# Loads reordered on one queue and stores moved to another in an mLSTM cell followed by a gelu MLP

## The chip, the cores and the metric

The kernel runs on one core of a Trainium2 chip. A core has TensorE (PE in the profile, with its weight loads as PEld), VectorE (DVE), ScalarE (ACT), GpSimd (POOL) and SyncE (SP), which here does nothing but issue DMAs. Matmuls read SBUF and write PSUM; the other engines move and change what lies there. The metric is the time of one execution on the device in microseconds. Four executions of the kernel before took 489.47 to 491.64 us, with a median of 490.15 us.

## What is computed

The first half is an mLSTM cell over 4 batches, 8 heads and 768 time steps, with heads of 40 elements. The second half is a two-layer MLP on the joined heads (3072 tokens of 320), with a sigmoid form of gelu between the layers:

```python
for t in range(S):
    m_new = np.maximum(f_gate[:, :, t] + m, i_gate[:, :, t])
    f_stab, i_stab = np.exp(f_gate[:, :, t] + m - m_new), np.exp(i_gate[:, :, t] - m_new)
    C = f_stab * C + i_stab * outer(vt, kt)
    n = f_stab * n + i_stab * kt
    y[:, :, t] = sigmoid(o_gate[:, :, t]) * (C @ qt) / np.maximum(np.abs(n @ qt), 1.0)
h = x @ w_in                       # 320 -> 2048
out = (h * sigmoid(1.702 * h)) @ w_out   # 2048 -> 320
```

The indices that broadcast the gates are left out here. The two weights arrive as 64-bit floats, and the kernel builds 32-bit ones from their bits.

## The kernel before

**Chunks.** Time is cut into six chunks `w` of 128 steps; within a chunk the recurrence is written as attention: scores of queries against keys (`scores`, L348 on TensorE), a weight matrix `wt` of gate products (`weights`), their product on VectorE (L350), values and the carried state (`values`, L360 and L365), the normalised output `y` (L380 to L390), its transpose into `xT` (`seam`, L399 on TensorE and the copy L400 on ScalarE), and the state's update (`new_states` L425, `carry` L433 and L435). The MLP then runs on the chunk's 512 tokens. While the MLP of chunk `w` runs on TensorE, the attention steps of chunk `w + 1` are put between its blocks, by the lists `blocks` and `stops` at the end of the kernel.

**The order is written by hand.** Each engine runs its instructions in the order in which the program lists them, and one that waits holds all behind it on that engine. The same holds for the DMAs issued on SP. Which instruction waits for what is worked out from the tiles that it reads and writes; a tile of a pool with two buffers (`o_sb`, say) can be written a third time only when the first one has been read.

**Loads.** Chunk 0 loads keys and queries as they lie and transposes them on TensorE. Later chunks load them in blocks of 32 rows (`load_blocks`, L117): 16 DMAs for the keys into `k_bl` and 16 for the queries into `q_bl`, eight of 64 KB and eight of 16 KB each. VectorE transposes those blocks (`transposes`, L302). `spread` (L317) copies a row of gate maxima from DRAM to all partitions of the four `wt` tiles. `load` (L105) fetches the o gates, v and k of a chunk with one DMA of 640 KB each.

**The weights** come in 20 pieces (`fetch`, L166): pieces 0 to 9 are `w_in`, 10 to 19 `w_out`, each in one to three DMAs. `convert` turns a piece into 32-bit floats with two instructions on ScalarE (L228, L229) and four on VectorE (L232 to L237). The table `beside` says at which step of chunk 0's MLP a piece is converted (`weights_in`) and which are fetched there, since their raw bits reuse the room of pieces converted before.

**The MLP of chunk 0** is plain: `up` (L458, L464) and, for the first two blocks, `full_rows` (L714, L737); the gelus are L468 and L765; then 16 blocks `down` (L561), for `n` = 0 to 3 and four batches. At `n` = 3 a batch is finished: VectorE copies PSUM into `o_sb` (L565) and SP stores it (L566). Block 12 to 15 are those four. From chunk 1 on, `up_fast` (L513, L541, with VectorE's sums L501 to L504 and adds L521) and `down_fast` (L610, L615, stores L619) compute the products with fewer matmuls, from sums of weights (`first_sums` L489, `weight_sums` L580) made beside chunk 0's MLP.

**The places that the change touches** are the start of the schedule (before `gate_out`), the step `j == 0` of chunk 0, the loads at `j == 4`, the place of `transposes(1, b)` among the `down` blocks, and the store in `down`.

Of the kernel before, what the change touches and what calls it, by code (L numbers as in the profile page):

```python
# [22 lines left out]
L = 128  # L23
# [11 lines left out]
def kernel(  # L35
# [12 lines left out]
    nc = tc.nc  # L48
    B, H, S, D = q.shape
# [44 lines left out]
    def load_gates(w):  # L94
        for dst, src in ((f_sb, f_gate), (i_sb, i_gate)):
            dst[w] = ld.tile([BH, L], FP, tag="fi", bufs=4, name="fi")
            nc.sync.dma_start(out=dst[w], in_=src[:, :, w * L:(w + 1) * L].rearrange("b h s -> (b h) s"))
# [10 lines left out]
    def load_blocks(w, which=slice(0, 2)):  # L108
        both = (k_bl, k), (q_bl, q)
        for dst, src in both[which] if isinstance(which, slice) else both[which:which + 1]:  # L110
            for two in range(2):
                for d in range(0, D, 32):
                    n = min(32, D - d)
                    r = two * 64 + d
                    for g in range(L // 32):
                        t = w * L + g * 32
                        nc.sync.dma_start(  # L117
                            out=dst[r:r + 32, :, g, 0:n],
                            in_=src[:, two:H:2, t:t + 32, d:d + n].rearrange("b j s d -> s (b j) d"))
# [36 lines left out]
    def fetch(n):  # L156
        if 6 <= n < 10:
            bits[n] = gp.tile([128, 512, 2], U32, tag="g", name="bits")
        else:
            room = xs if n == 19 else big[:, n if n < 6 else (n - 10) % 6, :]  # L160
            bits[n] = room.bitcast(U32).rearrange("p (a two) -> p a two", two=2)
        for r, c, src in pieces[n][1]:
            dst = bits[n][r, c].rearrange("p a two -> p (a two)")
            if len(src.shape) == 3:
                dst = dst.rearrange("p (j m) -> p j m", j=src.shape[1])
            nc.sync.dma_start(out=dst, in_=src)  # L166
# [18 lines left out]
    def keep_busy(n, pool=ps_a, tag="a"):  # L185
        p_idle = pool.tile([128, W], FP, tag=tag, name="p_idle")
        for _ in range(n):
            T.matmul(p_idle, idle, idle.unsqueeze(1).to_broadcast([128, 4, 128]), start=True, stop=True)
# [34 lines left out]
    def convert(n, engines="AV"):  # L223

        lo, hi, dst = bits[n][:, :, 0], bits[n][:, :, 1], pieces[n][0]
        dst_u = dst.bitcast(U32)
        if "A" in engines:
            A.activation(out=dst, in_=hi.bitcast(FP), func=AF.Abs)  # L228
            A.activation(out=lo, in_=lo, func=AF.Copy, scale=2.0 ** -29)  # L229
        if "V" not in engines:  # L230
            return
        V.tensor_scalar(out=dst, in0=dst, scalar1=HI_MIN, scalar2=HI_MAX, op0=OP.max, op1=OP.min)  # L232
        V.tensor_scalar(out=dst_u, in0=dst_u, scalar1=3, scalar2=0x3FFFFFFF, op0=OP.logical_shift_left,
                        op1=OP.bitwise_and)
        V.scalar_tensor_tensor(out=dst_u, in0=hi, scalar=0xC0000000, in1=dst_u, op0=OP.bitwise_and,
                               op1=OP.bitwise_or)
        V.tensor_tensor(out=dst_u, in0=dst_u, in1=lo, op=OP.add)  # L237
# [60 lines left out]
    def transposes(w, b):  # L298
        for bl, st, dst, name in ((k_bl, k_st, kT, "kT"), (q_bl, q_st, qT, "qT")):
            dst[w, b] = work.tile([128, NP, L], FP, tag=name, bufs=4, name=name)  # L300
            if w:
                V.transpose(out=dst[w, b].rearrange("p j t -> p (j t)"),  # L302
                            in_=bl[:, b * NP:(b + 1) * NP].rearrange("p j g c -> p (j g c)"))
                continue
            pt = ps_a.tile([128, NP, L], FP, tag="a", name="p_t")
            for p in range(NP):
                h = b * H + 2 * p
                T.transpose(pt[:, p, :], st[:, h:h + 2, :].rearrange("p a b -> p (a b)"), ident)
            if b == 0:
                keep_busy(1)  # L310
            A.copy(out=dst[w, b], in_=pt)
# [244 lines left out]
    def down(w, b, n):  # L556
        if n == 0:
            o_ps[w, b] = (ps_m if b < 2 else ps_x).tile([128, DM], FP, tag="mx"[b // 2], name="p_out")
        po = o_ps[w, b]
        for f in range(n * 4, n * 4 + 4):  # L560
            T.matmul(po, gs[w, f // 2][:, f % 2, b * L:(b + 1) * L], w_out_sb[:, f, :], start=(f == 0),  # L561
                     stop=(f == NF - 1))
        if n == NF // 4 - 1:
            o = op.tile([128, DM], FP, tag="o", name="o_sb")
            V.tensor_copy(out=o, in_=po)  # L565
            nc.sync.dma_start(out=out[b * S + w * L:b * S + (w + 1) * L, :], in_=o)  # L566

# [87 lines left out]
    def run(calls):  # L657
        for f, *args in calls:
            f(*args)


    def gate_out(b):
# [81 lines left out]
    def weights_in(n):  # L744
        done, ahead = beside.get(n, ((), ()))
        for p in done:
            convert(p)
        for p in ahead:
            fetch(p)
# [8 lines left out]
    for w in range(NW):  # L758
        more = w + 1 < NW
        for j in range(NF // 2):  # L760
            if w == 0 and j == 0:
                weights_in(0)
                for pair_ in range(2):
                    for i, g in enumerate(hidden_of(0, pair_)):
                        A.activation(out=g, in_=first[pair_][i], func=AF.Gelu_apprx_sigmoid)  # L765
            elif w == 0 and j % 2 == 0:
                weights_in(j // 2)
                up(j, j == 2)
            elif w and j % 4 == 0:
                up_fast(w, j, next_keys if more and j == 0 else None)  # L770
            if j == 0 and more:
                load(w + 1, "o")
            if w == 0 and j == 0:
                load_blocks(1, 0)
                spread(1)
            if w == 1 and j == 3:
                weight_sums(3)
            if more:
                if j == 4:
                    if w == 0:  # L780
                        load_blocks(1, 1)
                    load(w + 1, "v")
                    if w:
                        spread(w + 1)
                if j == (4 if w else 6):
                    load(w + 1, "k")
                if w and j == 3:
                    for b in range(2, 4):
                        transposes(w + 1, b)
            if w and j in (3, 7):  # L790
                hidden_sums(w, 0, (j // 4 * 2, j // 4 * 2 + 1), 1, 2)
                if j == 3:
                    hidden_sums(w, 0, (0, 1), 3, 4)
        side = attention(w + 1) if more else []
        if w == 0:

            blocks = [(lambda b=b, n=n: down(w, b, n)) for ns in ((0, 1), (2,), (3,)) for b in range(B) for n in ns]
            stops = (0, 1, 5, 7, 9, 11, 13, 15)
        else:
            blocks = down_fast(w, 0) + down_fast(w, 1)  # L800
            stops = (0, 1, 2, 4, 8, 10, 11, 12)
        for i, block in enumerate(blocks):
            if w == 0:
                weights_in(4 + i)
                if i == 0:
                    load_gates(2)
                if i == 2:
                    first_sums((0, 1))
                if i == 10:
                    load_blocks(2)  # L810
                for b in {2: (0, 1), 7: (2,), 9: (3,)}.get(i, ()):
                    transposes(1, b)
            elif w + 2 < NW and i == 0:
                load_gates(w + 2)
                load_blocks(w + 2)
            block()
            if i in stops and side:
                run(side.pop(0))
            if w == 1 and i == 1:
                weight_sums(2)  # L820
            if w:
                for at, c, *what in ((0, 0, (2, 3), 3), (1, 0, (2, 3), 4), (1, 1, range(4), 1),
                                     (5, 1, range(2), 2), (6, 1, range(2, 4), 2), (7, 1, range(4), 4)):
                    if i == at:
                        hidden_sums(w, c, *what)
                if i == 2 and not more:
                    hidden_sums(w, 1, range(4), 3)
            elif i in (12, 14):
                weight_sums(i // 2 - 6)
# [30 lines left out]
```

## Time and profile before

| | |
|---|---|
| median of 4 executions | 490.15 us (489.47 to 491.64) |
| profiled execution, its own time | 490.16 us |
| its span in the profile | 488.5 us |
| TensorE clock granted | 1.00 throughout |
| DMA over the span | 44.87 MB, 92 GB/s on average |
| DMA share, 0 to 40 us / 40 to 80 / 80 to 120 | 0.99 / 0.87 / 0.69 |

In the lines of the profile, a time is in microseconds from the start of the span, L-numbers are lines of the kernel, and `out<-in` are the names of the tiles. In a timeline the columns are start, length, engine, line, operation, tiles and count; a bracket at the end holds the idle time before the instruction and what ended it. In a table of waits each line is the engine, its tile and line, what it waited for, and then the total in microseconds, how often, and the longest. A wait for several things is put down to the one that came last by the profile; where the one named had long been done, it was another, often a DMA. SP's lines (SPq) are DMA issues: the length is that of the issue and not of the transfer.

### The profile page before, as it was taken

What the parts mean: (1) busy time and instruction counts of PE and PEld (TensorE: products, weight loads), DVE (VectorE), ACT (ScalarE), POOL (GpSimd) and SP (SyncE); (2) the same over time, 40 slices, a digit from 0 to 9 for tenths busy, and PEclk for the clock granted to TensorE, in tenths of its full rate; (3) what the DMA queues carried; (4) which work ended last, traced back from release to release, by engine and by line L of the source; (5) the groups of instructions that cost most, each with busy time, mean ns of one, the idle gap of its engine ahead of it and who ended that gap; (6) DMA issues with size and microseconds to landing.
All of it is one profiled execution on the core that took longest, in us unless ns stands there. A gap on an engine that the chain in (4) does not pass through costs nothing. (4 is left out here: it accounts for less than half of the span.)

```text
span 488.5 us, 10441 instructions
## 1 busy us (share of the span) xinstructions
PE 480.7 (98%) x4076; PEld 396.1 (81%) x4076; DVE 343.3 (70%) x855; ACT 221.2 (45%) x575; POOL 61.0 (12%) x103
## 2 busy tenths in 40 slices
PE   8999999999999999999999999999999999999997
PEld 4874456877688999787999877999977999977897
DVE  8789768887978965677776586686576786254831
ACT  6766766402458500476800474900364930255300
POOL 4030002231000340000322000232000120000000
PEclk9999999999999999999999999999999999999999
DMA  9999799663896200996100696300393000000000
GB/s 134 179 271 329 109 283 151 88 73 82 125 233 65 29 28 15 150 223 78 12 29 1 111 256 77 33 28 3 67 260 36 1 2 29 28 2 0 1 27 28
DMA packets 175953, 44.87 MB, mean 92 GB/s; under 512 B 164352, under 2 KB 169504, under 8 KB 175904
## 3 DMA queue, kind: packets, MB, share of 16 engines
q1 hardware_dynamic: 175904, 44.21, 48.5%
q8 instruction: 32, 0.52, 0.4%
q14 instruction: 17, 0.14, 0.1%
HBM read 40.17 MB, written 4.01 MB: 90 GB/s over the span
## 5 line engine op out<-in xcount | busy, mean ns | idle before, releaser
L610 PE MATMUL p_out<-w_out_sb,g 128*128 128x160 f32 x480 | 69.8, 301 | 0.0
L400 ACT COPY xT<-p_x 128x384 f32<-128x384 f32 x24 | 11.0, 480 | 127.3 <-PE p_x L399 127.3
L610 PEld LDWEIGHTS p_out<-w_out_sb,g 128*128 128x128 f32 x480 | 66.3, 190 | 0.9
L521 DVE TENSOR_TENSOR g<-p_u,g 128x256 f32<-128x256 f32 x80 | 33.7, 425 | 44.6 <-PE p_u L513 35.1
L518 ACT COPY g<-p_u 128x256 f32<-128x256 f32 x120 | 43.0, 377 | 43.7 <-PE p_u L513 39.5
L525 ACT ACTIVATE g<-g 128x256 f32<-128x256 f32 x120 | 42.3, 423 | 40.2 <-DVE g L521 40.2
L337 POOL TENSOR_SCALAR_AFFINE_SELECT wt<-wt 128x1024 f32<-128x1024 f32 x20 | 22.7, 1134 | 233.5 <-ACT wt L335 231.1
L615 DVE TENSOR_TENSOR o_sb<-o_sb,p_out 128x160 f32<-128x160 f32 x70 | 21.4, 318 | 42.2 <-PE p_out L610 41.8
L335 ACT ACTIVATE wt<-wt,cols 128x128 f32<-128x128 f32 x160 | 48.0, 391 | 0.0
L513 PE MATMUL p_u<-xT,w_in_sb 128*128 128x256 f32 x160 | 39.2, 383 | 0.3 <-DVE o_sb L565 0.3
L513 PE MATMUL p_u<-xs,big 128*128 128x256 f32 x160 | 37.9, 380 | 0.2 <-issue 0.2
L541 PE MATMUL p_v<-xT,w_in_x 64*128 64x512 f32 x80 | 37.2, 603 | 0.0
L541 PE MATMUL p_u<-xT,w_in_x 64*128 64x512 f32 x80 | 37.0, 602 | 0.0
L561 PE MATMUL p_out<-w_out_sb,g 128*128 128x320 f32 x128 | 36.2, 437 | 0.0
L350 DVE TENSOR_TENSOR wt<-p_s,wt 128x512 f32<-128x512 f32 x48 | 30.5, 684 | 7.5 <-POOL wt L337 5.5
L610 PE MATMUL p_out<-t,big 128*128 128x160 f32 x240 | 35.5, 301 | 0.0
L513 PEld LDWEIGHTS p_u<-xT,w_in_sb 128*128 128x128 f32 x160 | 29.6, 190 | 6.1 <-DVE o_sb L615 1.5
L513 PEld LDWEIGHTS p_u<-xs,big 128*128 128x128 f32 x160 | 29.9, 190 | 5.1 <-issue 0.6
L610 PEld LDWEIGHTS p_out<-t,big 128*128 128x128 f32 x240 | 33.3, 190 | 0.2
L561 PEld LDWEIGHTS p_out<-w_out_sb,g 128*128 128x128 f32 x128 | 23.8, 190 | 10.1 <-issue 0.5
L521 DVE TENSOR_TENSOR g<-p_v,g 128x256 f32<-128x256 f32 x80 | 29.8, 414 | 0.0
L541 PEld LDWEIGHTS p_v<-xT,w_in_x 64*128 64x128 f32 x80 | 14.1, 186 | 16.0 <-issue 16.0
(168 smaller groups left out, 862.2 us busy)
## 6 DMA issues: line engine op xcount, KB each, us to landing
wt<-m_row SPq DMA_DIRECT2D x20, 512.0 KB, 6.8
out_dram<-o_sb SPq DMA_DIRECT2D x24, 160.0 KB, 1.8
eo<-in_o_gate_dram SPq DMA_DIRECT2D x5, 640.0 KB, 5.5
v_st<-in_v_dram SPq DMA_DIRECT2D x5, 640.0 KB, 8.8
k_st<-in_k_dram SPq DMA_DIRECT2D x5, 640.0 KB, 11.8
big<-in_moe_w_in_dram SPq DMA_DIRECT2D x5, 512.0 KB, 7.0
k_bl<-in_k_dram SPq DMA_DIRECT2D x40, 64.0 KB, 2.7
q_bl<-in_q_dram SPq DMA_DIRECT2D x40, 64.0 KB, 2.7
```

The source lines that it names most:

```text
L335: A.activation(out=x[:, h, :], in_=x[:, h, :], func=AF.Exp, scale=-1.0, bias=cols[w][:, b * H + h:b * H + h + 1])
L337: G.affine_select(out=x, in_=x, compare_op=OP.is_ge, fill=0.0, base=0, pattern=[[0, H], [1, L]], channel_multiplier=-1)
L350: V.tensor_tensor(out=wt[w, b][:, :, i, :], in0=pw[i], in1=wt[w, b][:, :, i, :], op=OP.mult)
L400: A.copy(out=xT[w][:, :, b, :], in_=px)
L513: T.matmul(p[k][:, ts[t]], a[:, k // 2, k % 2 * 128:(k % 2 + 1) * 128], b, start=first, stop=True, skip_group_check=True)
L518: A.copy(out=g[k][i][:, ts[t]], in_=chain[k][:, ts[0]])
L521: V.tensor_tensor(out=g[k][i][:, ts[t]], in0=p[k][:, ts[pt]], in1=g[k][i][:, ts[t]], op=OP.add)
L525: A.activation(out=dst, in_=dst if src is None else src, func=AF.Gelu_apprx_sigmoid)
L541: T.matmul(p[k], w_in_x[r, k, :], x[r, 2, :], start=False, stop=True, skip_group_check=True)
L561: T.matmul(po, gs[w, f // 2][:, f % 2, b * L:(b + 1) * L], w_out_sb[:, f, :], start=(f == 0), stop=(f == NF - 1))
L610: T.matmul(po, a(f), b[:, f, :], start=(f == 0), stop=(f == NH - 1))
L615: V.tensor_tensor(out=dst, in0=x, in1=po, op=OP.add)
```

## The change

There are five edits. The keys of chunk 1 are loaded at the start, behind the first ten pieces of weights, instead of behind pieces 10 to 15. Its queries are loaded at step `j == 0`, before `spread(1)`, instead of at `j == 4`; the o gates of chunk 1 are loaded at `j == 4` instead of `j == 0`. The four stores of chunk 0 are issued by ScalarE and not by SP. Of the four first gelus, the two of the first block stand before the conversion of piece 5 (and the fetches of 10 to 15, which are on SP and not held by it), and the other two after it. Among the `down` blocks, the transposes of chunk 1 stand before `first_sums((0, 1))` and not after it, and at other blocks keep their place.

```diff
-            nc.sync.dma_start(out=out[b * S + w * L:b * S + (w + 1) * L, :], in_=o)
+            nc.scalar.dma_start(out=out[b * S + w * L:b * S + (w + 1) * L, :], in_=o)
...
     def run(calls):
         for f, *args in calls:
             f(*args)
+
+    load_blocks(1, 0)
...
             if w == 0 and j == 0:
-                weights_in(0)
                 for pair_ in range(2):
                     for i, g in enumerate(hidden_of(0, pair_)):
                         A.activation(out=g, in_=first[pair_][i], func=AF.Gelu_apprx_sigmoid)
+                    if pair_ == 0:
+                        weights_in(0)
...
-            if j == 0 and more:
+            if j == (0 if w else 4) and more:
                 load(w + 1, "o")
             if w == 0 and j == 0:
-                load_blocks(1, 0)
+                load_blocks(1, 1)
                 spread(1)
...
                 if j == 4:
-                    if w == 0:
-                        load_blocks(1, 1)
                     load(w + 1, "v")
...
                 if i == 0:
                     load_gates(2)
+                for b in {2: (0, 1), 7: (2,), 9: (3,)}.get(i, ()):
+                    transposes(1, b)
                 if i == 2:
                     first_sums((0, 1))
                 if i == 10:
                     load_blocks(2)
-                for b in {2: (0, 1), 7: (2,), 9: (3,)}.get(i, ()):
-                    transposes(1, b)
```

## The prediction

> **What bounds the kernel now.** I read the page first, then the waits by stretch, then the timelines of SP, VectorE and TensorE between 30 and 130 us.
>
> ```profile
> span 488.5 us, 10441 instructions
> ...
> PE 480.7 (98%) x4076; PEld 396.1 (81%) x4076; DVE 343.3 (70%) x855; ACT 221.2 (45%) x575; POOL 61.0 (12%) x103
> ...
> PE 14%; DVE 0%; issue 0%
> ```
>
> TensorE is busy for 98% of the span, and the chain that ended last is TensorE alone. What another engine saves is therefore worth only the TensorE time that it frees. Such time is found in two places. The waits of 60 to 90 us, and then those of 104 to 124 us, give them:
>
> ```profile
> DVE qT L302 <- DMA q_bl<-in_q_dram: 1.6, 1, 1.6
> ...
> PE p_s L348 <- DVE qT L302: 0.7, 1, 0.7
> ```
>
> ```profile
> DVE o_sb L565 <- PE p_c L425: 3.1, 1, 3.1
> ...
> PE p_u L513 <- DVE o_sb L565: 0.3, 1, 0.3
> ```
>
> The first: the second chunk's queries land late, their transpose waits, and the scores on TensorE wait 0.7 us. The second looks small, so I compare the same stage in two chunks on TensorE's timeline, from the first product of `up_fast` to the first of `down_fast`:
>
> ```profile
> 116.04 1.56 PE L513 MATMUL p_u<-xT,w_in_sb 128*128 128x256 f32 x6
> 117.95 0.70 PE L513 MATMUL p_u<-xT,w_in_sb 128*128 128x256 f32 x2 [0.35 <-DVE o_sb L565]
> ...
> 150.45 2.34 PE L610 MATMUL p_out<-w_out_sb,g 128*128 128x160 f32 x16
> ...
> 194.64 2.14 PE L513 MATMUL p_u<-xT,w_in_sb 128*128 128x256 f32 x8
> ...
> 226.74 2.34 PE L610 MATMUL p_out<-w_out_sb,g 128*128 128x160 f32 x16
> ```
>
> Chunk w=1 takes 150.45 - 116.04 = 34.41 us, chunk w=2 takes 226.74 - 194.64 = 32.10, and w=3 also 32.10 (270.92 to 303.02). So 2.31 us are lost in w=1, most of it inside matmuls that count as busy. VectorE's timeline says why, and SP's says what is behind it:
>
> ```profile
> 112.04 0.49 DVE L390 SCALAR_TENSOR_TENSOR y<-eo,den 128x320 f32<-128x320 f32 x1
> 115.60 0.49 DVE L565 COPY o_sb<-p_out 128x320 f32<-128x320 f32 x1 [3.07 <-PE p_c L425]
> ```
>
> ```profile
> 32.34 12.69 SPq L166 DMA_DIRECT2D big<-in_moe_w_out_dram  x14
> 45.18 0.38 SPq L105 DMA_DIRECT2D eo<-in_o_gate_dram  x1
> 45.60 14.56 SPq L117 DMA_DIRECT2D k_bl<-in_k_dram  x16
> 60.27 2.22 SPq L317 DMA_DIRECT2D wt<-m_row  x4
> 62.59 3.11 SPq L166 DMA_DIRECT2D big<-in_moe_w_out_dram  x5
> 66.79 10.77 SPq L117 DMA_DIRECT2D q_bl<-in_q_dram  x16
> ...
> 104.15 9.19 SPq L117 DMA_DIRECT2D q_bl<-in_q_dram  x16
> 113.44 4.82 SPq L566 DMA_DIRECT2D out_dram<-o_sb  x4
> ```
>
> The first output tile was copied at 106.07, but SP issues its store only at 113.44, behind the third chunk's query loads. It lands 2.1 us later, at 115.54. `o_sb` has two buffers, so the third copy (L565) starts at 115.60. The wait is put down to p_c, which the copy does not read; it is the store.
>
> **The stores.** Four DMA issues leave SP for ScalarE. An issue takes 0.33 to 0.43 us on SP; four on ScalarE are some 1.5 us, beside idle stretches of 6 to 7 us before its L400 copies. Each store now waits on ScalarE for its VectorE copy, and the copy of xT (L400) is queued behind it. The last store follows a VectorE copy that I put at 115 to 116; xT for that batch then comes at 115.9 to 117.3 instead of 115.27. Its first reader is VectorE's L501, behind `carry`, at 118, so this is covered; an xT after 118 would cost TensorE time one to one. No row shows what an issue costs on ScalarE; between nothing and 1 us, two to three times SP's, xT stays ahead of 118, and I take SP's 0.4.
> With stores issued at 108.5, the third copy could follow y at 112.5, and VectorE would reach L501 at 117.5 instead of 119.88. Its work then until the L521 adds (8.7 us) ends at 126.2, before TensorE wants them (126.4). All 2.31 us return: the upper end of the gain.
> One thing stands against it. SP never has more than eight transfers in flight: the piece issued at 32.34 left when the one eight before it (issued near 24.8, 7.3 us to landing) had landed, and those around it follow the same rule. If ScalarE's stores are counted in the same eight, the first must wait for the ninth query load of chunk 2, issued near 108.5 and 2.9 us to landing: 111.4. It lands at 113.5, VectorE is ahead by 115.6 - 113.5 = 2.1 us, and 2.0 us return. At worst the first store waits for the last query load (113.0 + 2.2 = 115.2) and lands at 117.3: a loss of about 1.8. I take -2.0.
> The Trainium skill (DMA: Bandwidth & Descriptors, "Issuing engines are not separate DMA queues") says that issuing from another engine saves only the sequencer's issue time, since all transfers share the same 16 DMA engines. By it the gain here is four issues of an SP that nobody waits for, 0, and the whole sum about -0.7. The row at 113.44 weighs more with me: what is saved is the place in line, 7 us.
>
> **The loads.** SP's order becomes: keys of chunk 1 (16), m_row, pieces 10 to 15 (14), queries (16), spread (4), pieces 16 and 17 (5), o gate, v, pieces 18 and 19, k. Bytes and count are the same; I work out landings.
> - Keys: the slots come free as the earlier pieces land, 31.0 to 41.3. The rest go at 0.53 to 0.57 us each (8.0 us for fifteen after 52.2; 9.15 for sixteen after 94.90): done near 46.5 to 47.
> - Pieces 10 to 15: 3.1 MB at the 380 GB/s of 64 to 70 us are 8 us, landings from 50.8 to 58. Piece 10's conversion on ScalarE moves from 49.60 to 50.8, piece 11's ends at 53.4, the gelu behind it (52.46) at 54.5. TensorE needs that PSUM at 56.8: nothing lost, 2.3 us of cover. Later conversions keep their times.
> - Queries: slots from 53.6, last issue near 63.4, landing 65.6 (79 before). Their transpose waits for no load.
> - Spread 63.5 instead of 60.27, so pieces 16 and 17 land 3.3 us later: piece 16 at 73.9 (70.6 before, where ScalarE waits 0.47). Its conversion stands on VectorE ahead of the transposes: 73.9 + 0.6 for the ScalarE half, + 2.4 for the VectorE half, + 1.3 for the first kT and qT gives 78.2. TensorE is ready at 79.16 and started at 79.86: **-0.7**. This needs piece 16 by 74.9.
> - The sums moved behind the transposes (L489, 1.22 + 1.99) end at 82.6. The score product on VectorE follows at 82.6 to 83.8 (81.13 to 82.33 before); TensorE wants it at 84.8. Covered by 1.0, else one to one. From there VectorE is full until 108 with about 0.6 to 2 us of slack against TensorE.
> - o gate and v, 160-byte packets, go at about 1000 per us (k: 4096 packets, 85.7 to 89.8): 8192 of them after piece 17 (its data end near 73.7) put v at 83.9 (83.8 before); needed at 84.8. Tanh waits for the o gate (79), and piece 17's conversion on ScalarE slips from 77.56 to 82.7, just in front of VectorE's need at 83.8.
> Piece 16 bounds it all. Earliest is 72, if no slot is ever late. Latest: pieces and queries take their whole old spells, 47 + 12.7 + 10.8 = 70.5, + 10.3 from spread to landing = 80.8. The low end is nearer, since the old spells hold waits for a backlog (6.6 us behind the o gate, 5.4 on earlier pieces) that is then not there.
>
> **Gelus before a conversion.** ScalarE's table load (1.28) starts at 33.9 instead of 35.39; the first gelus wait for TensorE (36.0), the conversion follows at 37.0. TensorE's start at 37.33 moves by at most 0.1; VectorE's conversion slips 0.6, covered by its wait of 0.59 at 49.16. I count -0.1 to +0.1, so 0.
>
> **Sum.** -2.0 - 0.7 = -2.7. The two overlap in part: the stores' time is set by SP's loads, not by TensorE, so with shared slots the 0.7 is given back at L521; with free ones both count (-3.0). I take -2.3. The profiled execution took 490.16 (span 488.5 and 1.7 around it), the median is 490.15: 490.15 - 2.3 = 487.85.
>
> **Rivals.**
> 1. *The stores gain nothing* (the pessimistic end above, or ScalarE held too long): then -0.7 at most, and a late v gives it back: 489.4 to 491. For it: the eight slots. Against: the store now has only loads before it that are issued by 109.
> 2. *Slower: piece 16 is late.* VectorE waits for it in front of the transposes, and the scores start 4.3 us after its landing. Past 75.6 each microsecond costs one; with the stores' 2.0 the balance is even at 77.6, and at 80.8 the sum is +3.2: 493.4. For it: eight slots filled with 32-row loads of 0.55 us each. Against: the same transfers in another order had all been issued by 83.9, so an order alone should move a piece by no more than what was put ahead of it.
> 3. *The order of loads is hidden entirely* (v or VectorE takes the 0.7 back) while the stores pay: -2.0, 488.15. This lies in the forecast's own range.
>
> **Numbers.** Forecast with rival 3: 0.58, from 486.9 (-3.2) to 488.6. Rival 1: 0.27. Rival 2: 0.15. A measurement here tells 0.3%, 1.47 us, from no change: faster below 488.68, slower above 491.62. So faster 0.58, same 0.27, slower 0.15. The range runs from 486.9 to 491.3; beyond lie most of rival 2 and a little below.
>
> **What would show it.** Right: stores issued by ScalarE between 108 and 112; the third L565 copy before 114; the w=1 stage near 32.1 to 32.5; no wait of L348 on qT; all after 150 shifted as a block. Wrong: ScalarE waiting on piece 16 past 75, TensorE waiting at L348 or L360 (v), a gelu waiting on pieces 10 or 11 near 53, or stores still issued after 113.

## The result and the profile after

The changed kernel takes 491.3 us (median of 46 executions, 488.07 to 494.83) against 490.26 us for the kernel before (70 executions, 489.05 to 496.38). The ratio is 1.0013, with a 95% interval of 0.9999 to 1.0027. The forecast was 487.85 us, a gain of 2.3. There was no gain. The profiled execution took 492.62 us, with a span of 490.9 and a mean granted clock of 0.996; the one before had 490.16, 488.5 and 1.000. In the experiments below, one execution of e1 (617.35 us) and one of e6 (551.26 us), at mean clocks of 0.754 and 0.852, are left out of every count and ratio.

The page of the changed kernel, span and busy times:

```profile
span 490.9 us, 10438 instructions
...
PE 481.5 (98%) x4076; PEld 398.0 (81%) x4076; DVE 342.7 (70%) x855; ACT 220.9 (45%) x575; POOL 61.7 (13%) x103
```

TensorE's waits between 50 and 124 us, its timeline at the places that the prediction named, and then two lines of the timeline before that the prediction does not show:

```profile
PE p_h L458 <- ACT g L468: 2.0, 1, 2.0
PE p_s L348 <- DVE qT L302: 1.3, 1, 1.3
```

```profile
58.96 5.40 PE L458 MATMUL p_h<-xT,w_in_sb 128*128 128x512 f32 x8 [1.96 <-ACT g L468]
...
69.75 2.32 PE L561 MATMUL p_out<-w_out_sb,g 128*128 128x320 f32 x8
...
84.50 1.16 PE L348 MATMUL p_s<-qT,kT 40*128 40x128 f32 x16 [1.34 <-DVE qT L302]
...
120.67 1.99 PE L513 MATMUL p_u<-xT,w_in_sb 128*128 128x256 f32 x8
...
152.90 2.34 PE L610 MATMUL p_out<-w_out_sb,g 128*128 128x160 f32 x16
```

```profile
65.74 2.32 PE L561 MATMUL p_out<-w_out_sb,g 128*128 128x320 f32 x8
...
79.86 1.16 PE L348 MATMUL p_s<-qT,kT 40*128 40x128 f32 x16 [0.70 <-DVE qT L302]
```

The first waits line is new, the second has nearly doubled (1.34 us against 0.70), and the wait of L513 for `o_sb` is gone. Read the starts against those before, in microseconds:

| place on TensorE | before | after | later by |
|---|---|---|---|
| first `down` block (L561) | 65.74 | 69.75 | 4.01 |
| first scores (L348) | 79.86 | 84.50 | 4.64 |
| first `up_fast` product of w=1 (L513) | 116.04 | 120.67 | 4.63 |
| first `down_fast` product of w=1 (L610) | 150.45 | 152.90 | 2.45 |
| end of the span | 488.5 | 490.9 | 2.4 |

So two things happened, of opposite sign. Up to the scores TensorE loses 4.6 us, and the w=1 stage gives back 2.18: it takes 152.90 - 120.67 = 32.23 us instead of 34.41. The difference of some 2.4 us stays to the end.

**The stores did what was forecast.** VectorE's and ScalarE's timelines, at the third output tile and at the stores:

```profile
116.67 0.49 DVE L390 SCALAR_TENSOR_TENSOR y<-eo,den 128x320 f32<-128x320 f32 x1
117.08 0.48 DVE L565 COPY o_sb<-p_out 128x320 f32<-128x320 f32 x1
```

```profile
112.32 2.24 ACTq L566 DMA_DIRECT2D out_dram<-o_sb  x2
114.60 0.48 ACT L400 COPY xT<-p_x 128x384 f32<-128x384 f32 x1 [8.76 <-PE p_i L365]
117.60 2.36 ACTq L566 DMA_DIRECT2D out_dram<-o_sb  x2
```

The third copy follows `y` with no wait; before it waited 3.07 us.

**The loads came late.** The gelus of block 4 on ScalarE before the change; then, after it, those gelus, the conversions of pieces 10, 11 and 16, and SP's issues:

```profile
52.46 1.08 ACT L468 ACTIVATE g<-p_h 128x512 f32<-128x512 f32 x2 [0.47 <-PE p_h L464]
```

```profile
54.20 0.67 ACT L228 ACTIVATE w_out_sb<-big 128x512 f32<-128x512 f32 x1 [4.42 <-DMA big<-in_moe_w_out_dram]
...
57.20 0.66 ACT L228 ACTIVATE w_out_sb<-big 128x512 f32<-128x512 f32 x1 [1.76 <-DMA big<-in_moe_w_out_dram]
...
58.33 2.04 ACT L468 ACTIVATE g<-p_h 128x512 f32<-128x512 f32 x4
...
80.09 0.66 ACT L228 ACTIVATE w_out_sb<-big 128x512 f32<-128x512 f32 x1 [5.96 <-DMA big<-in_moe_w_out_dram]
```

```profile
30.80 18.90 SPq L117 DMA_DIRECT2D k_bl<-in_k_dram  x16
...
50.33 7.89 SPq L166 DMA_DIRECT2D big<-in_moe_w_out_dram  x14
58.42 11.06 SPq L117 DMA_DIRECT2D q_bl<-in_q_dram  x16
69.52 1.91 SPq L317 DMA_DIRECT2D wt<-m_row  x4
71.53 3.65 SPq L166 DMA_DIRECT2D big<-in_moe_w_out_dram  x5
```

The gelus of block 4 stand behind the conversions of pieces 10 and 11 on ScalarE, so they start at 58.33 and not at 52.46, and TensorE wants their PSUM at 57.0. The transposes stand behind the conversion of piece 16 on VectorE, and the scores start 4.4 us after that piece lands. What the keys do to the DMA engines is seen in two stretches, the last two columns being the DMA share and GB/s; first after, then before:

```profile
42.00:44.00 2.00, 2.00 (x34) 1.04 (x27) 1.79 (x5) 1.71 (x4) 0.16 (x1) 1.00 0.14 15
44.00:46.00 2.00, 2.00 (x6) 0.87 (x5) 1.83 (x4) 0.65 (x2) 0.00 (x0) 1.00 0.51 30
```

```profile
42.00:44.00 2.00, 2.00 (x30) 0.96 (x23) 1.80 (x4) 0.69 (x3) 0.29 (x1) 1.00 0.96 314
44.00:46.00 2.00, 2.00 (x6) 0.87 (x5) 1.79 (x5) 0.57 (x2) 0.00 (x0) 1.00 0.98 316
```

While keys are being issued the engines move 15 and 30 GB/s (and 109 and 49 in the two stretches that follow); before, pieces moved there at over 310. One issue by one, the trace puts the lost time at the front of the 16: the first five keys' issues took 0.8 to 3.9 us each and the fifth ended at 43.2, while pieces 7 to 9 were still landing (the last at 43.9); of the other eleven, one took 1.1 us and the rest 0.49 each.

**A second loss that no term priced.** The stretches around the gelu wait after the change, the column ahead of the last two being the granted TensorE clock:

```profile
58.00:59.00 1.00, 0.04 (x1) 0.04 (x1) 0.93 (x3) 1.00 (x3) 0.00 (x0) 1.00 1.07 360
...
60.00:60.50 0.50, 0.50 (x2) 0.12 (x1) 0.34 (x1) 0.50 (x2) 0.00 (x0) 0.57 0.96 354
...
62.00:63.00 1.00, 1.00 (x2) 0.34 (x1) 0.86 (x2) 1.00 (x3) 0.00 (x0) 0.50 0.90 137
63.50:64.00 0.50, 0.50 (x2) 0.02 (x1) 0.47 (x2) 0.23 (x1) 0.00 (x0) 1.00 0.13 17
```

One microsecond after TensorE is back at work, its clock falls to half for some 3.4 us. That is why the eight L458 matmuls take 5.40 us where they took 3.7, and why 1.96 us of waiting have become 4.01 at the first `down` block.

The executions show the same thing without a profile. Their mean clock takes three values: 17 of the 46 have 0.999 or more (median 489.6 us), 22 have 0.996 or 0.997 (491.6), and 7 have 0.993 (493.5). A half clock of 3.4 us in 490 is a mean of 0.9965. So the groups are read as none, one and two such stretches at half clock (two can follow each other directly, as in the profiles of e3 and e15 below), and each costs about 1.9 us. Below, each such stretch is called a fall. The kernel before is not free of them: of its 102 executions that ran beside the experiments, 21 had one or two.

### The profile page after: what moved, and what is told of

Its sections match the earlier page's. It is cut to its first block, busy times and chain, and to the rows that moved or that the text cites. A ratio compares the mean times of both kernels' runs of the same rounds, so it can differ in the third digit from the quotient of the medians.

```text
span 490.9 us, 10438 instructions
## 1 busy us (share of the span) xinstructions
PE 481.5 (98%) x4076; PEld 398.0 (81%) x4076; DVE 342.7 (70%) x855; ACT 220.9 (45%) x575; POOL 61.7 (13%) x103
## 3 DMA queue, kind: packets, MB, share of 16 engines
HBM read 40.17 MB, written 4.01 MB: 90 GB/s over the span
## 5 line engine op out<-in xcount | busy, mean ns | idle before, releaser
L610 PE MATMUL p_out<-w_out_sb,g 128*128 128x160 f32 x480 | 69.8, 301 | 0.0
L610 PEld LDWEIGHTS p_out<-w_out_sb,g 128*128 128x128 f32 x480 | 66.3, 190 | 0.9
L513 PE MATMUL p_u<-xT,w_in_sb 128*128 128x256 f32 x160 | 38.9, 382 | 0.0
L513 PE MATMUL p_u<-xs,big 128*128 128x256 f32 x160 | 37.9, 379 | 0.0
L561 PE MATMUL p_out<-w_out_sb,g 128*128 128x320 f32 x128 | 36.2, 437 | 0.0
L610 PE MATMUL p_out<-t,big 128*128 128x160 f32 x240 | 35.5, 301 | 0.0
L513 PEld LDWEIGHTS p_u<-xT,w_in_sb 128*128 128x128 f32 x160 | 29.7, 190 | 5.4 <-DVE o_sb L615 1.5
L513 PEld LDWEIGHTS p_u<-xs,big 128*128 128x128 f32 x160 | 30.0, 190 | 4.6
L610 PEld LDWEIGHTS p_out<-t,big 128*128 128x128 f32 x240 | 33.3, 190 | 0.2
L561 PEld LDWEIGHTS p_out<-w_out_sb,g 128*128 128x128 f32 x128 | 23.8, 190 | 10.1 <-issue 0.5
L348 PE MATMUL p_s<-qT,kT 40*128 40x128 f32 x384 | 25.9, 280 | 1.3 <-DVE qT L302 1.3
```

The source lines that it names most:

```text
L348: T.matmul(pw[i][:, p, :], kT[w, b][r, p, :], qT[w, b][r, p, :], start=True, stop=True)
L513: T.matmul(p[k][:, ts[t]], a[:, k // 2, k % 2 * 128:(k % 2 + 1) * 128], b, start=first, stop=True, skip_group_check=True)
L610: T.matmul(po, a(f), b[:, f, :], start=(f == 0), stop=(f == NH - 1))
```

## The experiments

The kernels of one group (e1, e2, e3, e5; e4, e6, e7, e8; e10 to e12; e13 to e15) ran on the same chip, beside the kernel before. Ratios are against the kernel before, with 95% intervals. "Clock kept" counts executions with a mean clock of 0.999 or more.

| run | ratio | clock kept | piece 16 lands | scores start | wait there |
|---|---|---|---|---|---|
| the change | 1.0013 [0.9999, 1.0027] | 17 of 46 | 80.09 | 84.50 | 1.34 |
| e1, stores only | 0.9958 [0.9934, 0.9983] | 9 of 11 | | 80.94 | 0.93 |
| e2, all but the stores | 1.0051 [1.0028, 1.0075] | 5 of 12 | 79.71 | 84.13 | 3.49 |
| e5, keys back | 0.9962 [0.9928, 0.9996] | 6 of 12 | 75.58 | 80.00 | 0.66 |
| e3, gelus ahead of pieces 10, 11 | 1.0033 [1.0006, 1.0060] | 2 of 12 | 77.67 | 82.09 | 2.66 |
| e4, idle matmuls in the wait | 0.9983 [0.9953, 1.0014] | 9 of 12 | 77.82 | 82.33 | 1.92 |
| e8, transposes ahead of piece 16 | 0.9988 [0.9968, 1.0009] | 11 of 12 | 78.52 | 80.15 | none |
| e7, both ahead | 0.9975 [0.9952, 0.9998] | 9 of 12 | 77.06 | 78.84 | none |
| e6, keys back, transposes ahead | 0.9946 [0.9922, 0.9970] | 9 of 9 | 75.28 | 79.10 | none |

The times in the three columns on the right are those of the profiled execution, and piece 16's landing is read as the start of its conversion on ScalarE. The other executions can differ from the profiled one: e5 lost the clock in 6 of 12, though its profile has only one wait there, of 0.66 us, and full clock.

### e1: the stores alone

```diff
 (kernel before)
-            nc.sync.dma_start(out=out[b * S + w * L:b * S + (w + 1) * L, :], in_=o)
+            nc.scalar.dma_start(out=out[b * S + w * L:b * S + (w + 1) * L, :], in_=o)
```

> Only the four stores of chunk 0 go to ScalarE; all loads, gelus and transposes stand as in the kernel before. Theory (the two halves of the change are independent, the stores gain 2.2 us in the up_fast stage of w=1): 490.3 - 2.2 = 488.1, ratio 0.9955; that stage 32.1 to 32.4 us instead of 34.41; the scores still wait 0.7 us. Rival (the stage recovered because the loads had pushed TensorE 4.6 us back and so gave VectorE time): ratio 0.999 to 1.001, the stage near 34.

TensorE's timeline gives the stage:

```profile
117.11 1.99 PE L513 MATMUL p_u<-xT,w_in_sb 128*128 128x256 f32 x8
...
149.35 2.34 PE L610 MATMUL p_out<-w_out_sb,g 128*128 128x160 f32 x16
```

The stage takes 32.24 us, 2.17 less than before, and the time is 0.42% less, which is 2.1 us. This part of the change is a gain by itself.

### e2: the rest of the change

```diff
 (changed kernel)
-            nc.scalar.dma_start(out=out[b * S + w * L:b * S + (w + 1) * L, :], in_=o)
+            nc.sync.dma_start(out=out[b * S + w * L:b * S + (w + 1) * L, :], in_=o)
```

> The changed kernel with the stores of chunk 0 issued by SP again. Theory: the loads cost 4.6 us up to the end of chunk 0's MLP (2.0 waiting for a gelu, 2.0 at half the clock, 0.6 at the scores) and nothing gives it back: 494 to 495, ratio 1.007 to 1.010, in executions where the clock falls; some 2 us less where it does not. Rival (the stores' gain is only a shift of the loads' loss): ratio 1.001, as with the stores on ScalarE.

TensorE's timeline gives the stage again:

```profile
121.94 1.56 PE L513 MATMUL p_u<-xT,w_in_sb 128*128 128x256 f32 x6
...
156.28 2.34 PE L610 MATMUL p_out<-w_out_sb,g 128*128 128x160 f32 x16
```

The loss is there, 0.51% (2.5 us), though smaller than expected. It is split otherwise than expected, too: in the profile the gelu wait is 0.94 us with the clock kept behind it, the scores wait 3.49 us, and the clock is at half behind that (0.50 from 85 to 88 us). The stage is back at 156.28 - 121.94 = 34.34 us. The two parts multiply to 0.9958 x 1.0051 = 1.0009, within the interval of the whole change. So they add up, and no effect of one part on the other shows within the noise.

### e5: the keys back behind pieces 10 to 15

```diff
 (changed kernel)
-    load_blocks(1, 0)
...
             if w == 0 and j == 0:
-                load_blocks(1, 1)
+                load_blocks(1)
                 spread(1)
```

> The changed kernel with the keys of chunk 1 loaded at step j = 0 behind pieces 10 to 15 as before, the queries right after them. Theory (only the keys ahead of pieces 10 to 15 make pieces 10 and 11 late): pieces 10 and 11 come as in the kernel before, no wait for a gelu, full clock throughout, stores' gain kept, scores waiting 0 to 1.5 us for piece 16: 487.3 to 488.8, ratio 0.994 to 0.997, below both kernels. Rival (the later places of o gate, v and queries cost as much): ratio 1.000 or more, with TensorE waiting at the scores or the values for over 2 us.

SP's timeline of this run:

```profile
32.16 12.99 SPq L166 DMA_DIRECT2D big<-in_moe_w_out_dram  x14
45.31 10.85 SPq L117 DMA_DIRECT2D k_bl<-in_k_dram  x16
56.26 8.63 SPq L117 DMA_DIRECT2D q_bl<-in_q_dram  x16
64.94 1.92 SPq L317 DMA_DIRECT2D wt<-m_row  x4
66.94 3.72 SPq L166 DMA_DIRECT2D big<-in_moe_w_out_dram  x5
```

The same transfers stand ahead of piece 16 as in the changed kernel, in another order, and it is issued at 66.94 instead of 71.53. Keys, pieces and queries together take 32.7 us instead of 38.7: the keys' 16 issues take 10.85 us here and 18.90 there. The gelu wait is gone, and so is the loss. So the keys' place is the cause. In the six runs with the keys ahead their issues took 15.2 to 19.0 us, and all three kinds together 35.7 to 38.7; in the eight with the keys right behind the pieces (e5, e6, e10 to e15) it was 10.6 to 12.3, and 32.6 to 35.2. In the kernel before and e1, where the o gate stands between pieces and keys, the keys took 14.6 and 13.9.

### e3: the first gelus ahead of the conversions of pieces 10 and 11

```diff
 (changed kernel; `up` takes a call `between`, run behind the first gelu of the block)
         gelu(j)
+        if between:
+            between()
...
-    beside = {..., 2: ((9, 10, 11), (16, 17)), ...
+    beside = {..., 2: ((9,), ()), 'mid': ((10, 11), (16, 17)), ...
...
-                up(j, j == 2)
+                up(j, j == 2, (lambda: weights_in('mid')) if j == 4 else None)
```

> The changed kernel, with the conversions of pieces 10 and 11 (and the fetches of 16 and 17) put behind the first gelus of up(4) instead of ahead of them. Theory (ScalarE holds that gelu behind piece 10 and 11, and TensorE waits for the gelu's PSUM): no wait of L458 on a gelu near 57, no slice below full clock, the down blocks start near 65.8 instead of 69.75; what stays is the wait at the scores, 1 to 3 us now that TensorE comes earlier to it: 487.5 to 489.5, ratio 0.994 to 0.999. Rival (the loads slow TensorE in another way, by traffic): the stretch from 53 to 70 us stays some 16 us long, ratio 1.001.

TensorE's timeline:

```profile
66.01 2.32 PE L563 MATMUL p_out<-w_out_sb,g 128*128 128x320 f32 x8
...
82.09 2.08 PE L348 MATMUL p_s<-qT,kT 40*128 40x128 f32 x16 [2.66 <-DVE qT L302]
```

The first `down` block starts at 66.01, as before the change, so the gelu wait and its half clock are gone. The time is no better for it: the scores still start 4.42 us after piece 16 lands, and TensorE now waits for them twice as long, and the clock is down there (0.50 from 82 to 88 us, two falls in a row). Ten of twelve executions lost the clock, seven of them with two falls. The expectation of 0.994 to 0.999 missed: it had a wait of 1 to 3 us at the scores, but not that piece 16 alone sets their start, so that time won before it is lost there, nor the clock behind that wait.

### e4: idle matmuls in the gelu wait

```diff
 (changed kernel)
+        if j == 6:
+            keep_busy(6)
         full(j, True)
```

> Edit: as the changed kernel, but six matmuls on an idle tile (0.2 to 0.3 us each) fill TensorE's wait for the gelus of block 4, ahead of `up(6)`. They are no part of the result. Theory A (TensorE's wait of 1.96 us pulled the granted clock down to half for the 3.5 us behind it, and so made 4.0 us out of 2.0): the wait remains, the clock stays at 1.00 between 58 and 64 us, the eight L458 matmuls take 3.7 us instead of 5.4, and the down blocks start at 67.8 instead of 69.75. If the clock does not follow the idle time, they still start at 69.75. For the whole time there are two theories. Theory B (piece 16 alone sets the end: the scores start 4.4 us after it lands, whatever TensorE did before): the scores still start at 84.5, now after a wait of 3.3 us instead of 1.3, the time stays at the changed kernel's 491 (ratio 1.001 against the kernel before), or is up to 2 us longer if that longer wait now lowers the clock. Theory C (the gelu wait and its clock set the end): 2 us less, 489.3, ratio 0.997.

TensorE's timeline:

```profile
56.71 1.46 PE L188 MATMUL p_idle<-idle 128*128 128x512 bf16 x6
58.01 3.60 PE L458 MATMUL p_h<-xT,w_in_sb 128*128 128x512 f32 x8
...
82.33 1.16 PE L348 MATMUL p_s<-qT,kT 40*128 40x128 f32 x16 [1.92 <-DVE qT L302]
```

The clock stays at 1.00, but this does not decide theory A: in the profiled execution the gelus started at 56.32, so there was hardly a wait to fill. For theory B it speaks: TensorE stood ready at 80.4 and the scores started 4.5 us after piece 16. The time, 0.9983 with an interval from 0.9953 to 1.0014, holds both B and C. Nine of twelve executions kept the clock.

### e8: the transposes ahead of the conversion of piece 16

```diff
 (changed kernel, at the `down` blocks of chunk 0)
+                if i == 1:
+                    transposes(1, 0)
+                    transposes(1, 1)
                 weights_in(4 + i)
...
-                for b in {2: (0, 1), 7: (2,), 9: (3,)}.get(i, ()):
+                for b in {7: (2,), 9: (3,)}.get(i, ()):
```

> Edit: as the changed kernel, but the transposes of batches 0 and 1 of chunk 1 stand before the conversion of piece 16 instead of behind it. Theory B (in the changed kernel the wait of 1.34 us at the scores is piece 16's landing, through the conversion that stands ahead of the transposes on VectorE; without it the start is set by the gelu wait and the half clock before): the scores start when TensorE is ready, at 83.2 instead of 84.5, with no wait; the time is 1.3 us below the changed kernel, 490.0, ratio 0.9985 against the kernel before. Rival (piece 16 sets the end another way, through ScalarE's exponentials, which also stand behind its conversion): the scores start at 83.2 but the values after them wait for the product with the exponentials, and the time stays at 491.

TensorE's waits:

```profile
PE p_o L360 <- DMA v_st<-in_v_dram: 1.1, 1, 1.1
PE p_h L458 <- ACT g L468: 0.7, 1, 0.7
PE p_o L360 <- DVE wt L350: 0.5, 2, 0.3
```

The wait at the scores is gone, and the start no longer follows piece 16: it lands at 78.52 and the scores start at 80.15. The ratio is the expected one, but not by the expected road: the scores were to start at 83.2, behind a gelu wait with half clock, and that wait is only 0.72 us here, with the clock kept. A third wait has come up, which the wait at the scores had hidden until now: the values L360 wait 1.06 us for `v`, which lies behind pieces 16 and 17 on SP. Eleven of twelve executions kept the clock, with the gelu wait still there (its length is known for the profiled execution alone).

### e7: both out of the way, the keys still ahead

The edit is e3's and e8's together.

> Edit: keys still loaded ahead of pieces 10 to 15 as in the changed kernel, but both conversions are taken out of the way of what they held: 10 and 11 stand behind the first gelus of block 4 (as in e3), and the first two batches' transposes stand before the conversion of piece 16. Theory (a late piece costs time only through what is queued behind its conversion): no wait at the gelus and none at the scores, no half clock, the w=1 stage at 32.2, and the time is 0.7 below that of the stores alone: 487.5 to 488.5, ratio 0.994 to 0.996. Rival (the late loads cost time by themselves: the exponentials behind piece 16, the v and o gates behind it, or DMA traffic): a new wait at the values or at the pieces 17 to 19, and a ratio of 0.999 or more.

```profile
PE p_o L360 <- DMA v_st<-in_v_dram: 1.0, 1, 1.0
PE p_o L360 <- DVE wt L350: 0.5, 2, 0.3
```

Neither old wait is left, in TensorE's waits between 48 and 125 us, and the time is under that of the kernel before, but at 0.9975 [0.9952, 0.9998], above the expected 0.994 to 0.996, though the interval reaches into it. The rival was right in part: late loads also cost through `v` and through the product with the exponentials, 1.5 us here.

### e6: the keys back, the transposes ahead

The edit is e5's and e8's together.

> Edit: as e5 (keys back behind pieces 10 to 15, followed by the queries), and the transposes of batches 0 and 1 stand before the conversion of piece 16. Theory: e5's remaining wait of 0.66 us at the scores goes, since the queries have landed before 70 us; TensorE has no idle time of over 0.4 us between 50 and 110 us; profile span near 485.8, ratio 0.993 to 0.996. Rival (VectorE or the exponentials take the 0.66 back at the product with the scores): the same as e5, ratio 0.996.

TensorE has no wait that the profile lists between 48 and 150 us; the span is 485.6, and none of nine executions lost the clock. The ratio of 0.9946 is the lowest of all, below both the kernel before and the changed one; from e1 and e5 it is not told apart, as the intervals overlap. What is left of the change in it: the stores on ScalarE, and the queries straight behind the keys, so that they have landed (the last at 64.4) before the transposes' new place at 69.5.

### e10 to e12: a wait of a chosen length, put in the wrong place

```diff
 (e6, ahead of `full(6, True)` in `up`; n = 3, 4, 6)
+        if j == 6:
+            G.memset(xs[:, 512:1024], 0.0)
+            G.tensor_copy(out=xs[:, 0:512], in_=gs[0, 2][:, 0, :])
+            for _ in range(n):
+                G.affine_select(out=xs, in_=xs, compare_op=OP.is_ge, fill=0.0, base=-5000, pattern=[[1, 1024]],
+                                channel_multiplier=-1)
+            p_late = ps_a.tile([128, W], FP, tag="a", name="p_late")
+            T.matmul(p_late, idle, xs.bitcast(BF)[:, 0:W], start=True, stop=True)
```

> Edit: as e6 (which has no TensorE wait between 56 and 150 us), with one idle matmul ahead of `up(6)` that waits for a chain of one copy and three masks on GpSimd, idle otherwise there; it is no part of the result. Worked out: the chain starts at the first gelu of block 4's end (53.2), takes 0.6 + 3 x 1.13 = 4.0 us, TensorE reaches the place at 56.8, so the wait is 0.5 to 1.2 us. Theory (a wait costs its own length, and when it is long enough the granted clock falls to half for some 3.5 us behind it, which costs 1.7 to 2.0 us more and shows as a mean clock of 0.996 to 0.997): this one is too short; 0.5 to 1.2 us above e6, clock 1.000 in nearly all executions, ratio 0.996 to 0.997. Rival (the clock falls by itself, whatever TensorE does): the same share of executions below 0.998 in all three lengths.

> Edit: as e10 with four masks. The wait is 1.6 to 2.3 us, as long as the changed kernel's at the gelus. Theory: the clock falls in some of the executions, about half; those with the full clock 1.6 to 2.3 us above e6's full-clock ones, those with a mean of 0.996 to 0.997 another 1.7 to 2.0 us above; ratio 0.998 to 1.003. Rival (the clock falls by itself): a share as in e10 and e12.

> Edit: as e10 with six masks. The wait is 3.9 to 4.5 us, longer than the stretch of half clock itself. Theory: the clock falls in nearly all executions; 5.6 to 6.5 us above e6 in all, ratio 1.006 to 1.009. Rival (the clock falls by itself): 3.9 to 4.5 us above e6, ratio 1.003, and a share of falls as in e10.

```profile
PE p_late L477 <- POOL xs L474: 32.7, 1, 32.7
```

The three took 525.9, 526.9 and 528.5 us. Piece 19 is fetched into `xs` before this place in program order, so the chain waited for that load, and it overwrote the piece's raw bits (the last piece of `w_out` is not computed here). They say nothing on short waits. The line is e10's, and it shows a long one: TensorE went idle at 60.2, and the clock fell at about 63.7, 3.5 us into the idle time.

### e13 to e15: the same wait, ahead of that load

The same lines stand ahead of `weights_in(3)`, with n = 4, 5 and 7.

> Edit: as e6 (no TensorE wait between 56 and 150 us), with one idle matmul ahead of `up(6)` that waits for one copy (0.61 us) and four masks (1.08 us each) on GpSimd, which is idle then. They use the room `xs` before piece 19 is fetched into it, and are no part of the result. The chain starts at the first gelu of block 4's end, 53.1, and ends at 58.1; TensorE reaches the place at 56.8: a wait of 1.3 us. Theory D (a wait of TensorE costs its own length, and when enough of it falls into one stretch of some 3.4 us of the clock's own count, the granted clock is half for the next such stretch, which costs 1.7 to 2.0 us more and shows as a mean clock of 0.996 to 0.997): below 1.7, half of a stretch, it is too short; 1.3 us above e6's full-clock executions (487.3 to 490.3), and the clock falls in few executions, 0 to 3 of 12. Rival (the clock falls by itself, in whatever executions): the same share in all three lengths.

> Edit: as e13 with five masks; the chain ends at 59.2 and the wait is 2.4 us, a little over the changed kernel's at the gelus (1.96). Theory D: the clock falls in some executions and not in others, by where the wait lies in the clock's count, 3 to 9 of 12; those with the full clock are 2.4 us above e6, the others 4.1 to 4.4. Rival (by itself): a share as in the other two.

> Edit: as e13 with seven masks; the chain ends at 61.3 and the wait is 4.5 us. Theory D: longer than a whole stretch, so the clock falls in nearly all executions, 10 or more of 12, and the time is 6.2 to 6.5 us above e6. Rival (by itself): 4.5 us above e6, with a share as in the other two.

The waits came out longer than set, at 2.54, 3.99 and 6.33 us, since GpSimd's masks took 1.29 us each instead of 1.08 here. Read by their real lengths:

| run | wait | clock kept | one fall | two | median us | ratio |
|---|---|---|---|---|---|---|
| e6 | none | 9 of 9 | 0 | 0 | 488.77 | 0.9946 [0.9922, 0.9970] |
| e13 | 2.54 | 2 of 12 | 10 | 0 | 491.86 | 1.0004 [0.9984, 1.0024] |
| e14 | 3.99 | 1 of 12 | 8 | 3 | 493.22 | 1.0051 [1.0029, 1.0072] |
| e15 | 6.33 | 0 of 6 | 0 | 6 | 495.89 | 1.0095 [1.0067, 1.0124] |

e6 is from the other chip; the kernel before, on the same chip as e13 to e15, kept the clock in 20 of 23. The three shares hardly differ, as the rival had it, and theory D's 0 to 3 for e13 was for a wait of 1.3 us, which was not made. What speaks for the wait is the comparison with no wait (0 of 9) and with the kernel before (3 of 23), and the double falls, 0 of 12, 3 of 12 and 6 of 6 as the wait grows. So waits of 2.5 us and more bring the clock down in most executions. That shorter ones, or none, can do it too is not excluded, as the kernel before shows. The stretches of e13:

```profile
59.00:59.50 0.50, 0.00 (x0) 0.00 (x0) 0.50 (x1) 0.50 (x2) 0.50 (x1) 1.00 0.97 143
59.50:60.00 0.50, 0.30 (x1) 0.23 (x1) 0.50 (x1) 0.50 (x2) 0.14 (x1) 0.53 0.77 107
...
62.00:63.00 1.00, 1.00 (x2) 0.46 (x2) 0.97 (x3) 0.00 (x0) 0.00 (x0) 0.53 0.44 27
63.00:63.50 0.50, 0.50 (x2) 0.19 (x1) 0.47 (x2) 0.00 (x0) 0.00 (x0) 1.00 1.10 136
```

As in the changed kernel, the half clock lasts about 3.4 us. It begins here near 59.5, with TensorE idle since 57.2 and back at 59.7; in the changed kernel it began 1.1 us after TensorE was back. Within e13 the ten executions with a fall have a median of 491.9 us and the two without took 490.2 and 490.4: a fall costs some 1.6 us on top of the wait.

## Why the prediction was wrong

The step that failed is the loads' term. The scores were to start 0.7 us earlier, by a chain from the keys through pieces 10 to 15, queries and spread to piece 16; they started 4.64 us later. The parts one by one:

**Stores: right.** -2.0 was taken, and the stage gave -2.18, near the upper end of 2.31; e1 shows it alone. The Trainium skill (DMA: Bandwidth & Descriptors, "Issuing engines are not separate DMA queues") would have it that issuing from another engine saves sequencer time only, so 0 here. The measurement decides against that reading: what was saved was the place behind 16 loads on SP. The fear that the store would have to wait for the ninth query load came out the other way round; see the last section.

**Gelus ahead of a conversion: right.** TensorE's start at 37.33 moved to 37.41.

**Keys "done near 46.5 to 47": wrong, the first step that failed.** They were done at 49.7. The rate of 0.53 to 0.57 us held for the last eleven (6.4 us from 43.3 on). What failed is "the slots come free as the earlier pieces land", with the backlog "then not there": a free slot was not enough, since the first five issues took 0.8 to 3.9 us each behind pieces that were still landing, and only five keys were issued by 43.2. From there the delay grew: the pieces' issues ended at 58.2, when the queries were to have slots from 53.6, and the queries' last issue came at 69.5 instead of 63.4. The spread was put at 63.5 and came at 69.52; piece 16 was put at 73.9 and landed at 80.09. About half of the 6 us is the keys themselves, and the rest comes from the spells of the pieces and the queries, each longer than was worked out. And while the keys went out from 42 to 50, at 15 to 109 GB/s, no large piece was issued.

**Pieces 10 and 11, "nothing lost, 2.3 us of cover": wrong by size.** Piece 10's conversion came at 54.20 instead of 50.8 and the gelus at 58.33 instead of 54.5; 3.8 us late against 2.3 of cover leaves 1.5, and the trace has 1.96.

**Piece 16 "bounds it all": right, and rival 2 is what happened in the profile.** It said: scores 4.3 us after the landing, one for one past 75.6. Measured: 4.4. A landing at 80.09 then costs 80.09 - 75.6 = 4.5, less 2.0 for the stores makes +2.5, and the span grew by 2.4. Rival 2 had a chance of 0.15, because "an order alone should move a piece by no more than what was put ahead of it". e5 refutes that sentence: the same transfers ahead of piece 16, and 4.5 us between the two landings. (With the keys ahead it landed at 77.1 to 80.1 in six profiles, so the changed kernel's own is the latest; in e5 and e6 it landed at 75.6 and 75.3.) That the median ended at 491.3, close to rival 1's 489.4 to 491, is no support for rival 1: the stores did gain, and the loads lost as much.

**The gain of 0.7 at the scores: not there.** Its condition, piece 16 by 74.9, was not met in any run with the keys ahead, and not in e5 (75.58) or e6 (75.28) either. In e6 the wait goes because the transposes no longer stand behind that piece.

**v "at 83.9, needed at 84.8": wrong, and hidden.** e7 and e8 show `v` arriving 1.0 and 1.1 us after it is wanted.

**The clock: left out altogether.** No term priced a wait of TensorE at more than its length. By the groups of executions the falls come to (22 + 2 x 7) x 1.9 / 46 = 1.5 us on average. This and the time that full-clock executions spent waiting took back what the stores gave. Those full-clock executions, at 489.6, are 1.0 us under the 490.6 that the 81 full-clock executions of the kernel before had beside the experiments (not the same groups of runs); the median of all is not under.

Three things stay open. Why an issue takes up to 3.9 us when keys stand behind pieces of `w_in` is not tested by a run; the trace only shows where that time goes. Which of the changed kernel's two waits brings the clock down is not settled: e3, without the first, lost it in 10 of 12, and e8, without the second, in 1 of 12, which points to the wait at the scores, but in the changed kernel's own profile it fell behind the gelu wait. And why e5 lost it in 6 of 12, with 0.66 us of waiting in its profile, is not shown; the waits of the other executions are not on record.

## What to carry to other kernels

When loads are reordered on one queue, follow each later transfer to the instruction that needs it and list what stands behind that instruction on its engine: here two conversions of weights held gelus and transposes that needed none of those weights. Removing the first of several waits in a row gained nothing in e3, while a later one was set by another late transfer of the same queue, so look for all of them before building. Price a TensorE wait of some 2 us or more at its length plus 1.6 to 1.9 us for the clock that may follow, and do not take a shorter one for safe: the kernel before and e5, with 0.7 us in their profiles, lost the clock at times.

## What was not expected of the hardware

- A wait of 1.96 us between busy stretches was followed by half the granted clock for 3.4 us, and with a wait of 2.54 us this was so in 10 of 12 executions. In profiled executions, waits of 2.66 (e3) and 3.49 us (e2) had it as well, and waits of 0.94 (e2) and 1.92 us (e4) did not. The Trainium skill (TensorE: Matmul & The Clock Gate, "Part 1: The HAM clock gate") describes a window of about 3.4 us that runs freely, and half rate after at least one idle window. The length of the half clock agrees with that window; its start does not need a whole idle one: in e13 it came some 2.4 us into the wait. In the 3.4 us ahead of the fall TensorE had been idle for 1.96 us in the changed kernel, and for some 2.2 in e3, 2.4 in e13, 2.8 in e2 and 3.2 in e14 (estimates from the clock in stretches of 0.25 us). A window that counts as idle when it is partly so would fit this and the scatter, but no run shows the count itself.
- The loads on SP waited for the stores on ScalarE. The third chunk's query loads took 15.88 us to issue in the changed kernel and 15.18 in e1, against 9.19 in the kernel before and 9.30 in e2, where SP issues the stores. In the changed kernel's trace no more than eight transfers of the two engines together are in flight, and the third of those loads is issued at 115.25, just after the first store has landed at 115.23. It cost nothing, since the first transpose that reads them starts at 128.5. SP's waits between 100 and 130 us:

```profile
SPq L117 <- DMA out_dram<-o_sb: 7.0, 3, 5.1
```

- GpSimd's masks over 128 x 1024 took 1.08 us each while VectorE was idle (e10) and 1.28 to 1.32 us each while VectorE was converting weights (e13 to e15, VectorE busy for 96% of that time).
